# A delta-rule attention with an MLP behind it on one core: chunk 2's Gram matrix moves into its own activation buffer, chunk 0's masked products alternate row halves, and the first third of the instruction order is rearranged

## The chip, the cores and the metric

The kernel runs on one core of one Trainium2 chip. The metric is the device time in microseconds (us) of one launch. The kernel before was timed three times; the median is 257.81 us, and the runs lie between 257.49 and 259.07 us.

## What is computed

Four batches of eight heads hold sequences of 768 tokens with 48 features. Each head keeps a 48 x 48 state that every token reads and then corrects; the outputs of all heads go through a two-layer MLP (384 to 2048 to 384) with the tanh form of GELU.

```python
k_n = k / (np.linalg.norm(k, axis=-1, keepdims=True) + 1e-06)
for t in range(S):
    y[:, :, t] = q[:, :, t] @ state            # per batch and head
    v_old = state.T @ k_n[:, :, t]
    state = state + beta[t] * outer(k_n[:, :, t], v[:, :, t] - v_old)
x = y.transpose(0, 2, 1, 3).reshape(B * S, H * D)
out = gelu_tanh(x @ w_in) @ w_out
```

## The kernel before, in words

**Tiling.** The 768 tokens are cut into 12 chunks of 64. A chunk has two units (x = 0, 1), so there are 24 units; a unit holds 16 of the 32 batch-and-head pairs, eight of them over each half of the 128 partitions. Names in the text are operation.unit or operation.chunk: A4.0 is operation A4 of unit 0, V.0 is V of chunk 0.

**Stages of a chunk.** The recurrence inside a chunk becomes the inverse of a triangular 64 x 64 matrix per head.
- Loads (`load`, L473): four DMAs each of k, q and v. `norms` (L496 to L504): squares (sq), their sums (sum), root (pow), eps, reciprocal (inv).
- `prep`: normalised keys (kn or knc, L532 and L525) and queries (qb, qbc) as bf16, their transposes by TensorE (Tk, Tq, or T for both) and the copies out of PSUM (kTk, kTq, kT), the Gram matrix of the keys (GD or G, L565), its copy dn (L344), and the masked product of keys and queries (wq, or wqa with wqb).
- `leaf`: the 8 x 8 diagonal blocks are inverted by elementwise operations. F (L645) folds dn, lp and x0 start, L (L661) spreads, and then six pairs xm, xa (L667, L670) follow each other on DVE. xb multiplies the result with beta (bc, copied out by betaC).
- `scale`: xe or xec (L603, L600) spreads xb over a block-diagonal tile zt; GM makes the masked products, for chunk 0 directly from dn and zt (`direct`, L618 and L619), later from the keys by way of KZ and kz; lw (L635) selects from GM.
- `invert`: X10, X11 build the block-diagonal tile bd, and A4, rt4, B4, A5, rt5, B5 with copies into bd (bde40, bde41 or xi4 with bdc; be50, be51) raise it to the inverse of the whole chunk.
- `chain`: the one serial path from chunk to chunk, V, K, R, U, Un, S, Sn, and for the output Q, O, On; then the transpose of the output (X, xT, or a DMA, turnx).
- `mlp`: 16 products up (L837), four GELUs of four each (L841), 8 groups of four products down (L848), two copies Z and the stores.

**What sets the order.** A text table ORDER lists all operations in one sequence; `:p a d g s` names the engine (TensorE, ScalarE, VectorE, GpSimd, SyncE) and `@` the first PSUM bank. `Flow.order` deals the list out to the engines' queues, which run strictly in that order. `Flow.emit` gives each instruction waits on semaphores for those operations whose result it reads, whose buffer it overwrites, or whose PSUM bank it takes. GpSimd's operations on the upper and the lower half of the partitions also wait for one another. DMAs are issued by SP, ACT and GpSimd at their place in these queues. `fillN` is a 128 x 512 product of zeros whose result nobody reads; 37 of them stand in the table.

**Buffers.** dn, the bf16 copy of the Gram matrix, has two buffers that alternate by chunk (`dn[c % 2]`). gT, the activations of the MLP, has three (`gT[c % NG]`), each 16 x 256 elements per partition.

## Time and profile before

| What | Value |
|---|---|
| median of three runs | 257.81 us |
| the profiled execution, its own time | 256.19 us |
| its span from the first to the last instruction | 254.5 us |
| PE, DVE, ACT, POOL busy | 230.0, 186.5, 154.6, 136.6 us |
| first product up (up8.0) starts at | 48.86 us |

The profile lists engine time by line of the code. PE is TensorE's matmuls, PEld its weight loads, DVE VectorE, ACT ScalarE, POOL GpSimd, SP SyncE; a q behind a name is the queue that issues DMAs. A busy share is a mean over stages with different limits, so the stages are read one by one. DVE instructions that don't depend on each other overlap by up to 0.1 us in the records, so that the sum of their durations is a little more than the time that passes.

### The profile page before, as it was taken

What the parts mean: (1) busy time and instruction counts of PE and PEld (TensorE: products, weight loads), DVE (VectorE), ACT (ScalarE), POOL (GpSimd) and SP (SyncE); (2) the same over time, 40 slices, a digit from 0 to 9 for tenths busy, and PEclk for the clock granted to TensorE, in tenths of its full rate; (3) what the DMA queues carried; (4) which work ended last, traced back from release to release, by engine and by line L of the source; (5) the groups of instructions that cost most, each with busy time, mean ns of one, the idle gap of its engine ahead of it and who ended that gap; (6) DMA issues with size and microseconds to landing.
All of it is one profiled execution on the core that took longest, in us unless ns stands there. A gap on an engine that the chain in (4) does not pass through costs nothing.

```text
span 254.5 us, 12234 instructions
## 1 busy us (share of the span) xinstructions
PE 230.0 (90%) x5488; PEld 176.2 (69%) x5499; DVE 186.5 (73%) x448; ACT 154.6 (61%) x242; POOL 136.6 (54%) x160
## 2 busy tenths in 40 slices
PE   0286887799999999999999999999999999999994
PEld 0256656687776868777778787777786778678672
DVE  5896899998678989878888878898494765655100
ACT  0625757887577779768737687643958425436261
POOL 8646348977195397718257988463535526230000
PEclk9998999999999999999999999999999999999999
DMA  5999978989565679785777627687358220222042
GB/s 96 181 168 159 197 135 135 169 139 109 81 82 104 121 131 138 148 173 94 140 130 158 124 43 136 127 161 136 59 105 181 37 49 4 53 48 64 3 93 62
DMA packets 105332, 28.45 MB, mean 112 GB/s; under 512 B 99392, under 2 KB 104512, under 8 KB 105280
## 3 DMA queue, kind: packets, MB, share of 16 engines
q1 hardware_dynamic: 90288, 22.17, 50.8%
q0 software_dynamic: 2880, 3.15, 8.0%
q10 hardware_dynamic: 12112, 2.35, 6.2%
q8 instruction: 43, 0.70, 1.1%
q14 instruction: 9, 0.07, 0.1%
HBM read 20.64 MB, written 4.72 MB: 100 GB/s over the span
## 4 chain that ended last, share of the span: by engine, by line
PE 70%; DVE 13%; SPq 5%; POOL 3%; ACT 3%; DMA 2%; issue 2%; DVEq 0%
PE ps L848 24%; PE ps L837 22%; PE ps L705 5%; SPq L473 4%; PE ps L765 2%; DMA qraw<-in_q_dram 2%; PE ps L612 2%; PE ps L565 2%; PE ps L710 2%; ACT gT L841 2%; PE ps L772 2%; PE ps L645 2%; PE ps L786 2%; PE ps L628 1%; DVE lw L635 1%
## 5 line engine op out<-in xcount | busy, mean ns | idle before, releaser
L837 PE MATMUL ps<-xT,W 128*128 128x256 bf16 x576 | 75.2, 273 | 0.5 <-ACT gT L841 0.5
L848 PE MATMUL ps<-W,gT 128*128 128x384 bf16 x384 | 72.9, 326 | 0.0
L841 ACT ACTIVATE gT<-ps 128x1024 bf16<-128x1024 f32 x48 | 48.6, 1023 | 22.1 <-PE ps L837 21.7
L837 PEld LDWEIGHTS ps<-xT,W 128*128 128x128 bf16 x576 | 51.2, 97 | 8.7 <-ACT gT L841 0.6
L848 PEld LDWEIGHTS ps<-W,gT 128*128 128x128 bf16 x384 | 33.9, 97 | 18.2
L695 POOL TENSOR_SCALAR_AFFINE_SELECT bd<-lw 64x512 bf16<-64x512 bf16 x31 | 20.7, 672 | 27.6 <-DVE lw L635 23.3
L717 DVE TENSOR_TENSOR rl<-ps,two 128x384 bf16<-128x384 f32 (+1 forms) x48 | 22.8, 486 | 8.6 <-PE ps L705 8.2
L635 DVE CAST_PREDICATED lw<-mlw,ps 128x832 bf16<-128x832 uint16 x24 | 24.4, 1020 | 5.0 <-PE ps L612 4.8
L500 POOL TENSOR_TENSOR nrm<-nrm,half 128x16 f32<-128x16 f32 x9 | 26.7, 2969 | 1.6 <-DVE nrm L498 1.6
L344 ACT ACTIVATE bd<-ps 32x256 bf16<-32x256 f32 (+1 forms) x38 | 15.8, 424 | 8.9 <-PE ps L710 5.4
L705 PEld LDWEIGHTS ps<-lw,bd 128*128 128x128 bf16 x384 | 14.9, 96 | 5.4 <-DVE bd L697 1.0
L705 PE MATMUL ps<-lw,bd 128*128 128x48 bf16 (+1 forms) x384 | 16.8, 180 | 1.6 <-DVE bd L697 0.5
L735 POOL COPY bd<-xi 64x256 f32<-64x256 f32 x20 | 8.1, 403 | 16.3 <-ACT xi L344 8.4
L344 ACT ACTIVATE ob<-ps 128x384 f32<-128x384 f32 x17 | 8.3, 489 | 13.3 <-PE ps L848 13.2
L603 POOL TENSOR_TENSOR zt<-xb,blk 128x1024 bf16<-128x1024 bf16 x7 | 13.8, 1984 | 4.5 <-DVE xb L682 4.3
L670 DVE TENSOR_TENSOR xl<-ps,xl 128x96 bf16<-128x96 f32 (+3 forms) x66 | 14.7, 227 | 1.7
L667 DVE TENSOR_TENSOR ps<-ps,xl 128x96 f32<-128x96 f32 (+5 forms) x66 | 14.4, 221 | 2.1 <-PE ps L661 0.4
L350 ACT ACTIVATE kT<-ps 128x512 bf16<-128x512 f32 x16 | 9.3, 596 | 7.5 <-PE ps L628 7.5
L532 POOL TENSOR_TENSOR tok<-kraw,nrm 128x384 bf16<-128x384 f32 x7 | 7.2, 1032 | 11.4 <-DVE nrm L504 6.4
L600 POOL TENSOR_TENSOR zt<-xb,blk 128x2048 bf16<-128x2048 bf16 x3 | 10.9, 3641 | 4.1 <-DVE xb L682 3.9
L587 POOL TENSOR_TENSOR wq<-wq,muq 128x512 bf16<-128x512 bf16 x11 | 12.8, 1171 | 0.4
L344 DVE CAST bd<-ps 32x256 bf16<-32x256 f32 (+1 forms) x21 | 8.8, 422 | 5.3 <-ACT bd L344 3.1
(144 smaller groups left out, 441.2 us busy)
## 6 DMA issues: line engine op xcount, KB each, us to landing
out_dram<-ob SPq DMA_DIRECT2D x22, 192.0 KB, 3.1
vraw<-in_v_dram SPq DMA_DIRECT2D x43, 96.0 KB, 3.6
qraw<-in_q_dram SPq DMA_DIRECT2D x40, 96.0 KB, 3.6
kraw<-in_k_dram SPq DMA_DIRECT2D x38, 96.0 KB, 3.5
W<-in_moe_w_in_dram POOLq DMA_DIRECT2D x2, 768.0 KB, 8.6
W<-in_moe_w_out_dram POOLq DMA_DIRECT2D x2, 768.0 KB, 8.7
qraw<-in_q_dram ACTq DMA_DIRECT2D x8, 96.0 KB, 3.7
kraw<-in_k_dram ACTq DMA_DIRECT2D x6, 96.0 KB, 4.0
```

What stands on the lines that cost most here:

```text
L344: return e.activation(out, in_, ACT.Copy) if e is nc.scalar else e.tensor_copy(out, in_)
L500: if e is nc.scalar else e.tensor_tensor(nr[:, 1, hx], nr[:, 0, hx], half[:, hx], ALU.pow), reads=[nrn, "half"] + ["one"] * (c < ROOTS),
L603: A(("dve", "pool"), op("xe"), lambda e, P: e.tensor_tensor(zt[m][:, :, :].rearrange("p h (b j) -> p h b j", j=LB), xb[y][:, H * x:H * x + ...
L635: A(("dve",), op("lw"), lambda e, P: e.copy_predicated(lw[m][:, :, 0:LW - LB], mlw[:, :, :].rearrange("p w t -> p (w t)")[:, 16:16 + LW - ...
L667: A(("dve",), f"xm{m}.{c}", lambda e, P, m=m, w=w, part=part: e.tensor_tensor(part(P), P(f"L.{c}")[:, off[m]:off[m] + 2 * H * w].rearrange ...
L670: A(("dve",), f"xa{m}.{c}", lambda e, P, m=m, part=part: e.tensor_tensor(xl[y][:, :, m + 1:LB], part(P), xl[y][:, :, m + 1:LB], ALU.add), ...
L695: A(("pool", "dve"), op(f"X1{a}"), lambda e, P, src=lw[m][hf(a), :, LW - C:LW], dst=bd[b_][hf(a), :, hf(a)], a=a: e.affine_select(out=dst, ...
L705: ins = e.matmul(P(name)[:, C * h + c0:C * h + c1], bd[b_][:, h, :], rhs[:, h, :])
L717: A(("dve",), op(f"rt{i}"), lambda e, P, i=i, c0=c0, c1=c1, r_=r_: e.tensor_tensor(r_[:, 0:H, c0:c1], P(ps(f"A{i}")).rearrange("p (h t) -> ...
L837: ins = e.matmul(P(ph)[:, 256 * f:256 * f + 256].rearrange("p (x t) -> p x t", x=2), W1[:, j, 128 * (i + f):128 * (i + f) + 128], x_[:, :, ...
L841: A(("act",), f"gelu{i // 4}.{c}", lambda e, P, i=i, ph=ph: e.activation(g_[:, i:i + 4, :], P(ph).rearrange("p (f t) -> p f t", f=4), ACT. ...
L848: ins = e.matmul(P(po)[:, 0:DM], g_[:, f, 128 * b:128 * b + 128], W2[:, f, :], start=(f == 0), stop=(f == FC - 1))
```

## The change

The changed kernel computes the same. Four things differ in the code.

1. Chunk 2 writes its Gram matrix dn into the first quarter of gT[2], the buffer that later takes chunk 2's own activations, and not into dn[0], which chunk 0 has used. `dn` of units 4 and 5 then no longer waits for the readers of chunk 0's dn; the first GELU of chunk 2 gets a write dependence on it.
2. `direct`, the masked products of chunk 0, visits the two row halves (a) in turn instead of one half after the other.
3. bc of chunk 0 is copied without a change of sign, and xb.0 becomes the plain product that the other chunks use, so that GpSimd may take it.
4. ORDER differs. Up to the start of chunk 3 nearly every operation has another place, some another engine, form or bank; later the engines' queues differ in smaller steps and in the banks. 31 fills remain of 37.

```diff
 ORDER = """
-k1.00:a tmplz:g k0x1.11:s ident:g bdz1:d blk1:g blk2:g bdz3:d k0x1.01:a q0.00:s low1:d rowz:d ...
+v0.01:a k0x1.00:s pad1:g pad5:d pad0:g mmlw:d low1:d rpad0:g one:d tmplz:d half:d wz:g ...
...
-                    A(EV, f"betaC{i}", lambda e, P, i=i, d0=d0, d1=d1, w=w: neg(
+                    A(EV, f"betaC{i}", lambda e, P, i=i, d0=d0, d1=d1, w=w: (neg if i else copy)(
...
+        gram_of = [(dn[c % 2], c % 2) if c != 2 else (gT[2][:, 0:4, :].rearrange("p f (h t) -> p (f h) t", t=C), 2) for c in range(NC)]
...
-            d_, dnn = dn[c % 2][:, H * x:H * x + H, :], f"dn{c % 2}{x}"
+            d_, dnn = gram_of[c][0][:, H * x:H * x + H, :], f"dn{gram_of[c][1]}{x}"
...
             def direct(e, P):
                 for g in range(4):
-                    for p, a in quad:
+                    for p in range(2):
                         h, o_ = 4 * p + g, 512 * p + 2 * C * g
-                        e.matmul(P(ps("GM"))[hf(a), o_ + LW - C:o_ + LW - LB], zt[m][hf(a), h, hf(a)], d_[hf(a), h, 0:C - LB])
-                        ins = e.matmul(P(ps("GM"))[hf(a), o_:o_ + C - 16], d_[hf(a), h, :], zt[m][hf(a), h, C * a + 16:C * a + C])
+                        for a in range(2):
+                            e.matmul(P(ps("GM"))[hf(a), o_ + LW - C:o_ + LW - LB], zt[m][hf(a), h, hf(a)], d_[hf(a), h, 0:C - LB])
+                        for a in range(2):
+                            ins = e.matmul(P(ps("GM"))[hf(a), o_:o_ + C - 16], d_[hf(a), h, :], zt[m][hf(a), h, C * a + 16:C * a + C])
...
-            A(("dve",) if c == 0 else ("dve", "pool"), f"xb.{c}", lambda e, P: e.scalar_tensor_tensor(xb[y][:, :, :], xl[y][:, :, :], -1.0, bc[:, c, :, :], op0=ALU.mult, op1=ALU.mult) if c == 0 else
-              e.tensor_tensor(xb[y][:, :, :], xl[y][:, :, :], bc[:, c, :, :], ALU.mult),
+            A(("dve", "pool"), f"xb.{c}", lambda e, P: e.tensor_tensor(xb[y][:, :, :], xl[y][:, :, :], bc[:, c, :, :], ALU.mult),
...
-                  reads=["one"], frees=[ph], writes=[f"{gn}.{i // 4}"])
+                  reads=["one"], frees=[ph], writes=[f"{gn}.{i // 4}"] + ([f"dn2{x}" for x in range(2)] if c == 2 and not i else []))
```

`leaf` folds from `gram_of[c]` in the same way. How the instructions moved is shown at three places. Lines of the changed kernel are one to three higher than those of the kernel before.

**VectorE's queue at the very start.** bd are the block-diagonal tiles that have to be cleared once, kraw0 the raw keys of chunk 0, sq1 and nrm their squares and norms, tok0 the normalised keys (kraw1 those of chunk 1). Before:

```order
L422 MEMSET bd1 128x512
L422 MEMSET bd3 128x512
L397 MEMSET low0 128x1
L382 MEMSET rows0 128x512
L422 MEMSET bd0 128x512
L365 TENSOR_SCALAR identf0<-tmpl0 32x32
L422 MEMSET bd4 128x512
L344 COPY lw1<-tmpl0 128x896
L422 MEMSET bd5 128x512
L395 TENSOR_REDUCE unit0<-ident0 128x8
L497 TENSOR_TENSOR sq1<-kraw0 128x384
```

Now:

```order
L423 MEMSET bd0 128x512
L383 MEMSET rows0 128x512
L405 MEMSET tok0 128x16x8
L396 TENSOR_REDUCE unit0<-ident0 128x8
L366 TENSOR_SCALAR identf0<-tmpl0 32x32
L498 TENSOR_TENSOR sq1<-kraw0 128x384
L499 TENSOR_REDUCE nrm0<-sq1 128x8
L392 TENSOR_TENSOR own0<-blk0 128x64
L402 CAST xl0<-unit0 128x16
L405 MEMSET tok0 128x16x8
L393 TENSOR_TENSOR sel0<-ident0,own0 128x1024
```

Four of the five clears of bd have left the stretch ahead of the keys (bd1, bd3, bd4 and bd5 are GpSimd's now). The tile sel stands behind the first sum of squares and now behind own and blk, which GpSimd writes.

**VectorE's queue at the end of the first leaf.** xl0 and xl1 are the leaves of chunks 0 and 1, zt0 the spread tile, kT the copies of transposed queries, lw the selected products, bd0 and bd1 the tiles to invert. Before:

```order
L681 SCALAR_TENSOR_TENSOR xb0<-xl0,bc0 128x128
L603 TENSOR_TENSOR zt0<-xb0,blk0 128x1024
L344 COPY kT3<-ps 128x512
L667 TENSOR_TENSOR ps<-ps,xl1 128x16
L603 TENSOR_TENSOR zt0<-xb0,blk0 128x1024
L344 COPY kT2<-ps 128x512
L670 TENSOR_TENSOR xl1<-ps,xl1 128x16
L603 TENSOR_TENSOR zt0<-xb1,blk0 128x1024
L635 COPY_PREDICATED lw0<-mlw0,ps 128x8x104
```

Now:

```order
L673 TENSOR_TENSOR xl0<-ps,xl0 128x16
L351 TENSOR_SCALAR bc0<-ps 128x512
L601 TENSOR_TENSOR zt0<-xb0,blk0 128x2048
L684 TENSOR_TENSOR xb1<-xl1,bc0 128x128
L604 TENSOR_TENSOR zt0<-xb1,blk0 128x1024
L638 COPY_PREDICATED lw0<-mlw0,ps 128x8x104
L638 COPY_PREDICATED lw1<-mlw0,ps 128x8x104
L699 TENSOR_TENSOR bd0<-lw0,two0 64x8x64
L345 CAST gT2<-ps 128x512
L719 TENSOR_TENSOR rl0_0<-ps,two0 128x8x48
```

xb.0 has gone to GpSimd, both halves of its spread are one instruction, the copies kT have gone to ScalarE, betaC3 (bc0) and the Gram copy of unit 5 (gT2) have come from ScalarE, and unit 0 is inverted ahead of unit 1.

**ScalarE's queue from the chain of chunk 0 to the first GELU.** us0, st1 and xo0 are the results of U, S and O; L872 (L874 now) loads the table for the GELU. Before:

```order
L350 ACTIVATE rs0<-ps 128x768
L344 ACTIVATE bd1<-ps 32x8x32
L344 ACTIVATE bd0<-ps 32x8x32 x2
L344 ACTIVATE us0<-ps 128x768
L344 ACTIVATE bd3<-ps 64x8x64
L347 ACTIVATE bd3<-ps,low0 128x8x64
L344 ACTIVATE st1<-ps 128x768
L344 ACTIVATE xT0<-ps 128x768
L872 ACT_TABLE_LOAD
```

Now:

```order
L874 ACT_TABLE_LOAD
L874 ACTIVATE one0<-one0 128x1
L345 ACTIVATE bd1<-ps 64x8x64
L348 ACTIVATE bd1<-ps,low0 128x8x64
L351 ACTIVATE rs0<-ps 128x768
L345 ACTIVATE bd0<-ps 32x8x32 x2
L345 ACTIVATE bd1<-ps 32x8x32 x2
L345 ACTIVATE us0<-ps 128x768
L345 ACTIVATE xo0<-ps 128x2x8x48
L345 ACTIVATE st1<-ps 128x768
```

The table load stands ahead of the inversion of unit 1, On.0 (xo0) and the fourth copy of B5 (be51.1) have come from VectorE, and xT.0 has gone to VectorE.

## The prediction

> **What bounds the kernel now.** First I read the stretches of the span.

> ```profile
> core 0: us, PE busy (x) PEld busy (x) DVE busy (x) ACT busy (x) POOL busy (x), PEclk, DMA share, GB/s
> 0.00:20.00 20.00, 8.10 (x116) 5.20 (x117) 14.68 (x44) 6.59 (x13) 13.52 (x36) 1.00 1.14 149
> 20.00:48.90 28.90, 22.54 (x611) 17.14 (x620) 26.27 (x79) 19.45 (x38) 18.22 (x23) 0.94 0.98 156
> 48.90:60.00 11.10, 10.93 (x264) 8.96 (x264) 9.49 (x17) 8.44 (x12) 9.61 (x9) 1.00 1.00 139
> 60.00:100.00 40.00, 38.42 (x1093) 29.39 (x1090) 33.07 (x80) 30.81 (x52) 23.89 (x26) 1.00 0.67 110
> 100.00:240.00 140.00, 139.06 (x3338) 107.82 (x3338) 101.97 (x228) 84.46 (x126) 71.38 (x70) 1.00 0.54 100
> ```

> The columns are length, busy time of the five engines with their counts, granted clock and DMA. From 48.9 us on PE is idle for 0.17, 1.58 and 0.94 us in 191 us: that stage is a fixed sum of matmuls, and no other engine sets its end. Before it PE has gaps, some of its work is fills, and DVE is busy for 26.27 of 28.90 us. So the run ends a fixed time after the first product up, and what counts is when that starts. The chain of waits over this stretch says what leads there.

> ```profile
> 14.46 6.23 DMA qraw<-in_q_dram
> ...
> 20.71 0.36 DVE tok L344
> ...
> 34.33 0.94 DVE lw L635
> ...
> 46.35 0.82 DVE xo L344
> ...
> 48.93 1.09 PE ps L837 x9
> ```

> It comes out of the load of chunk 0's queries, which was issued at 14.46 and landed at 20.69, and then runs through DVE nearly without a break until the products up. DVE's other waits up to there:

> ```profile
> DVE tok L344 <- DMA qraw<-in_q_dram: 1.8, 1, 1.8
> ...
> DVE sq L497 <- DMA kraw<-in_k_dram: 0.9, 1, 0.9
> ```

> DVE is idle for 48.9 - 14.68 - 26.27 = 7.9 us before the first product up. The start of that product is therefore DVE's work ahead of it, plus these waits. Both sets of matmuls behind up8.0 are the same in the two orders but for A5.3 (it now stands behind) and three fills (two ahead of it now, one new one behind).

> **The change part by part.** *DVE's queue.* I compare what stands ahead of the products up, before with kz.4 as the next instruction, now with xT.0 included, since up8.0 now waits for it there. Prices are the means of groups up to 49 us:

> ```profile
> L603 DVE TENSOR_TENSOR zt<-xb,blk 128x1024 bf16<-128x1024 bf16 x4 | 2.8, 690 | 0.6 <-POOL xb L682 0.5
> L422 DVE MEMSET bd<- 128x512 f32 x5 | 2.4, 485 | 1.2 <-PEq L902 1.0
> ...
> L344 DVE COPY kT<-ps 128x512 bf16<-128x512 bf16 x5 | 2.1, 417 | 0.0
> ...
> L532 DVE TENSOR_TENSOR tok<-kraw,nrm 128x384 bf16<-128x384 f32 x3 | 1.6, 556 | 0.1
> L344 DVE CAST dn<-ps 128x512 bf16<-128x512 f32 x2 | 1.3, 680 | 0.0
> L697 DVE TENSOR_TENSOR bd<-lw,two 64x512 bf16<-64x512 bf16 x3 | 1.3, 419 | 0.1
> ...
> L344 DVE CAST xo<-ps 128x768 bf16<-128x768 f32 x1 | 1.0, 951 | 0.0
> ...
> L350 DVE TENSOR_SCALAR kT<-ps 128x512 bf16<-128x512 f32 x1 | 0.7, 692 | 0.1
> ...
> L344 DVE CAST bd<-ps 32x256 bf16<-32x256 f32 x1 | 0.4, 416 | 0.0
> ```

> and, for the two forms that come later in the run:

> ```profile
> L525 DVE TENSOR_TENSOR tok<-kraw,nrm 128x768 bf16<-128x768 f32 x2 | 1.9, 950 | 0.0
> L600 DVE TENSOR_TENSOR zt<-xb,blk 128x2048 bf16<-128x2048 bf16 x1 | 1.2, 1227 | 0.0
> ```

> Out: four clears of bd less one that comes ahead, 3 x 0.485 = 1.46; four copies kTq, 4 x 0.417 = 1.67; On.0 0.95; be51.1 0.42; three of X less two, 0.42; kn.2 and kn.3 as one knc.1, 2 x 0.556 - 0.950 = 0.16; xe.0 and xe.1 as one xec.0, 2 x 0.690 - 1.227 = 0.15; qb.1, bdc40.0 and rt5.3, together 1.15. Sum 6.38 us. In: dn.1 and dn.5, 2 x 0.680 = 1.36; betaC3, priced as the nearest copy of its size out of PSUM, 0.69; kn.0 0.56; xT.0, 768 elements of bf16, which is not in the rows of DVE and must cost more than the 0.417 of 512 elements and less than the 0.951 of 768 wider ones (I take 0.55, by the row of its type); small clears, templates and own, 0.9. Sum 4.06 us. DVE's work ahead of the first product falls by 2.3 us.

> *DVE's waits.* They do not stay as they are. The first keys come later: the last quarter of them is fifth in ACT's queue before, sixth in SP's now, at one issue per 0.68 us.

> ```profile
> 0.80 6.11 ACTq L473 DMA_DIRECT2D kraw<-in_k_dram  x9
> ...
> 6.60 0.99 DVE L497 TENSOR_TENSOR sq<-kraw 128x384 f32<-128x384 f32 x1 [0.93 <-DMA kraw<-in_k_dram]
> ```

> 0.79 + 5 x 0.68 = 4.2 against 0.80 + 4 x 0.68 = 3.5, so sq.0b starts at some 7.2 in place of 6.60, and the clears that filled the time ahead of it are gone. That puts about 2.6 us of idle time there (bounds 1.9, if the landing at 6.60 was not set by this quarter, and 3.0). Against that the wait of 1.8 for the queries goes: all four loads are issued by 11 us, three us earlier, and GpSimd converts them (bound: none of it goes, if the loads then land no earlier). The wait for xb.1 on GpSimd (0.5) goes as xb.1 comes to DVE; xb.0 on GpSimd is covered by betaC3's 0.69. A new one stands ahead of rt4.0: X10.0 waits on GpSimd behind xe.2 and a clear, and A4.0 behind it.

> ```profile
> 31.78 2.42 POOL L603 TENSOR_TENSOR zt<-xb,blk 128x1024 bf16<-128x1024 bf16 x1
> ```

> 2.42 + 0.5 + 0.7 = 3.6 us, and about 0.4 for A4.0 and the hand-offs, against 0.69 + 2 x 1.02 + 0.42 + 0.68 = 3.8 of DVE's own work with overlaps of 0.3: some 0.5 us is left (0 to 1.5). Waits in all: +2.6 - 1.8 - 0.5 + 0.5 = +0.8, rounded down to +0.7 for the smaller hand-offs that the merged spread saves. Net at the first product: -2.3 + 0.7 = -1.6 us, from 48.86 to 47.3.

> *Alternating row halves.* Two batches of `direct` and two of the later kind:

> ```profile
> L618 PE MATMUL ps<-dn,zt 64*64 64x56 bf16 x32 | 1.4, 192 | 0.2 <-ACT kT L344 0.2
> ...
> L612 PE MATMUL ps<-kT 48*64 48x56 bf16 x32 | 0.8, 194 | 0.4 <-ACT kT L350 0.4
> ```

> A batch takes 0.7 us now and could take 0.4, as the batch whose neighbours lie in different row halves does. I count nothing: DVE's xb.1 and xe.3 (1.0 us) cover GM.0, and lw.0 covers GM.1. Without that cover it saves 0.3 us once.

> *The room for chunk 2.* dn.5 started at 33.97 behind G.5, after the readers of chunk 0's buffer had ended at 32.3, and the order still has the GM of chunk 0 ahead of G.4: nothing, with nothing to cover.

> *ACT and PE.* ACT takes On.0 and the fourth copy of B5, and the table load leaves the path to the first GELU; it has 9.4 us free in the second stretch. A5.3 now costs 0.3 us behind up8.0, where PE is full, and the balance of fills gives back 0.2. Total: -1.6 + 0.1 = -1.5 us.

> *A rule against it.* The change has GpSimd and DVE work side by side more often. Two rows bear on that:

> ```profile
> 47.07 3.10 POOL L500 TENSOR_TENSOR nrm<-nrm,half 128x16 f32<-128x16 f32 x1
> ...
> 49.58 0.93 DVE L603 TENSOR_TENSOR zt<-xb,blk 128x1024 bf16<-128x1024 bf16 x1
> ```

> A DVE product of two tensors took 0.93 under a GpSimd one, 0.69 beside the start of xe.2. [...] Were that third added to knc.1, kn.1, kn.0 and xe.3, the gain would be 0.6 us instead of 1.5; xe.3 under xe.2 shows none of it, so the sum leaves it out.

> **The rivals.** *More is gained (about 3 us).* If the first keys are no later (idle 0.7 less), the wait ahead of rt4.0 is covered (0.5 less) and GM.0 shows its 0.3: -3.0, and the median is 254.8. For it: the keys share DMA engines that are busy anyway. Against it: the issue alone is 0.7 later.

> *The start eats it (no change, 257.8).* On PE Tq.1 stands ahead of Tk.0, GD.1, GD.0 and F.1, so that late queries now hold the Gram matrix too; and DVE has betaL1 and sum.2 ahead of the whole leaf, sum.2 needing keys of chunk 2 that ACT issues behind sq.0a. If either keeps 1.6 us of the old wait of 1.8, nothing is left. For it: the one load whose flight shows took 6.23 us. Against it: it was issued at 14.46, behind more traffic.

> *TensorE drops to half clock inside the inversions (slower, 259.4).* It has happened once here, between 20 and 30 us:

> ```profile
> 20.00:25.00 5.00, 3.27 (x68) 3.07 (x70) 3.86 (x14) 2.89 (x8) 3.55 (x8) 0.81 1.15 155
> 25.00:30.00 5.00, 4.50 (x65) 3.37 (x63) 4.72 (x25) 3.18 (x7) 1.47 (x1) 0.84 1.11 201
> ...
> 21.81 0.56 PE L457 MATMUL ps<-bhl,rows 128*128 128x48 bf16 x16
> ...
> 25.02 1.49 PE L457 MATMUL ps<-bhl,rows 128*128 128x16 bf16 x32
> ```

> 16 matmuls took 0.75 there against 0.56, for a shorter form: at least 0.2 per batch. Between A4.0 and X.0 some 15 batches stand in one line: 15 x 0.2 = 3.0, and -1.5 + 3.1 = +1.6. It ends slower than before once more than seven of them fall into it. There are six fills fewer; against it, PE is no emptier there than before, when the clock stayed at 1.00. [...]

> **How the numbers follow.** The profiled execution took 256.19 us, its span 254.5; the forecast for such an execution is 254.7, for the span 253.0. It lies 1.6 under the median, so the median goes from 257.81 to 256.3. Chances: forecast 0.50, more gained 0.20, start eats it 0.20, half clock 0.10. With all costs at their bad bounds (idle 0.4 more at the keys, the wait of 1.8 kept, 1.0 more at rt4.0, 0.4 on xT.0, against -1.5) the time is 259.9, with all at the good ones 254.6; I leave out the corners and give 254.2 to 259.2. A measurement of this kernel tells a change of about 1% (2.6 us) from none, that is 255.2 and 260.4. Most of the second case and the lower edge of the first lie below: faster 0.28. The worst of the half clock lies above: slower 0.08. Within 1%: 0.64.

> **What would show it.** Right: the first product up at 47.3 (46.5 to 48.1); DVE's wait for the queries gone and about 2.6 us of idle time ahead of sq.0b, near 7.2; DVE busy for some 39 us ahead of that product; PE idle for under 3 us between it and the last 15 us. Wrong: an xm1.1 later than 23.5, a granted clock under 1 after 30 us, or a PE that waits for ACT between 47 and 60 us.

## The result, and the profile after

The changed kernel is slower by about 1%: 260.6 us median of 15 runs (258.64 to 261.95) against 258.05 us for the kernel before on the same chips (255.56 to 259.11); ratio 1.0106, 95% interval 1.0071 to 1.014. I had forecast 256.3, with a range up to 259.2. The profiled execution took 260.2 us, its span 258.5 (before 256.19 and 254.5). Ratios here and below are taken over the fast runs alone, those within 1.5% of the kernel's fastest, so that they can differ a little from the quotient of the medians.

The stretches of the span of the changed kernel, as before them in the prediction:

```profile
core 0: us, PE busy (x) PEld busy (x) DVE busy (x) ACT busy (x) POOL busy (x), PEclk, DMA share, GB/s
0.00:20.00 20.00, 7.93 (x68) 4.26 (x69) 12.61 (x39) 5.50 (x11) 13.82 (x37) 1.00 1.09 150
20.00:48.90 28.90, 20.24 (x524) 15.92 (x530) 23.50 (x71) 17.73 (x34) 16.51 (x21) 0.82 0.77 125
48.90:60.00 11.10, 9.40 (x227) 7.32 (x230) 9.28 (x21) 7.19 (x11) 7.77 (x9) 1.00 0.92 141
60.00:100.00 40.00, 38.83 (x1097) 30.43 (x1096) 32.67 (x80) 29.61 (x47) 25.45 (x27) 1.00 0.74 119
100.00:240.00 140.00, 139.22 (x3458) 108.96 (x3460) 105.78 (x236) 86.66 (x129) 74.43 (x74) 1.00 0.58 104
```

From 60 us on nothing has changed: TensorE (PE) is idle for 1.17 and 0.78 us. The loss lies ahead of it. Between 20 and 48.9 us VectorE (DVE) is busy 2.8 us less than before, and the clock is 0.82 and not 0.94. The chain of waits names the place:

```profile
34.67 0.42 PE ps L566 x16
35.19 1.95 issue
37.14 0.32 PE ps L631 x13
37.49 0.60 ACT kT L351
...
43.48 0.56 DVE rl L719
...
52.42 0.57 DVE xT L345
53.03 0.83 PE ps L839 x6
```

The first product up starts at 53.03; it was at 48.86 before, and I had forecast 47.3. From there to the end of the span 205.5 us pass, before 205.6: the whole loss of 4.2 us is made by 53 us. That is the difference of two single executions; the medians differ by 2.6 us, and the profiled execution of the kernel before lies 1.9 us under its median. So the figures below say where the time of these executions went, and the ratios say what an edit is worth. In the chain stands a piece of 1.95 us called issue, in which TensorE waited for nothing that the profile shows. Its own timeline there:

```profile
34.67 0.42 PE L566 MATMUL ps<-kT 48*64 48x128 bf16 x16 [0.25 <-issue]
34.97 0.22 PE L631 MATMUL ps<-zt,tok 64*64 64x64 bf16 x3
37.14 0.29 PE L631 MATMUL ps<-zt,tok 64*64 64x64 bf16 x13 [1.95 <-issue]
38.14 0.61 PE L428 MATMUL ps<-wz 128*128 128x512 bf16 x2 [0.71 <-ACT kT L351]
```

L631 is KZ.3, sixteen small products without a semaphore between them. TensorE stops after the third. A wait on another engine cannot stand there; what is left is that the next instruction was not there. Two more such gaps follow, inside GM.4 (1.02 us, until 55.02) and inside S.1 (0.78 us, until 70.04). The kernel before has no such gap of over half a microsecond inside an operation. The profile's list of DMA queues and two windows of the DMA view show the supply; the columns are packets, megabytes and share of the 16 engines. First the whole execution, then 30.7 to 34.7 us, then 34.7 to 35.0 us:

```profile
q8 instruction: 43, 0.70, 1.1%
```

```profile
q0 software_dynamic: 312, 0.64, 92.8%
q1 hardware_dynamic: 333, 0.06, 9.7%
```

```profile
q0 software_dynamic: 26, 0.05, 93.2%
q8 instruction: 1, 0.02, 19.2%
q1 hardware_dynamic: 27, 0.01, 15.8%
```

43 fetches bring 0.70 MB, 16 KB each, and TensorE has 10,976 loads and products, 255 to a fetch: I take these for its instructions, fetched in blocks. The gaps fit that: from the end of the first to the end of the second TensorE makes 758 loads and products, from there to the end of the third 762, and three fetches start in each of these stretches. With TensorE's semaphore instructions, of which the trace has 80, it is 764 and 768, and by this I estimate a block at 256 instructions. From 30.7 to 34.7 us, while q0, the weight load w1.1, holds 93% of the DMA engines, no fetch moves. One starts at 34.73, 0.46 us before TensorE stands still, and 2.4 us after its start TensorE goes on.

Behind the gap the clock falls:

```profile
35.00:40.00 5.00, 2.04 (x66) 1.41 (x62) 2.02 (x5) 3.05 (x6) 2.67 (x5) 0.93 0.64 115
40.00:45.00 5.00, 4.65 (x148) 3.72 (x137) 4.14 (x10) 3.56 (x7) 2.26 (x3) 0.50 0.85 151
45.00:50.00 5.00, 3.72 (x84) 2.70 (x87) 4.51 (x16) 3.62 (x8) 4.02 (x5) 0.88 0.65 89
```

TensorE is busy for 2.04 of the 5 us around the gap, and then runs at half clock from 39.3 to 46.2, through both inversions. The trace's record of the clock runs in steps of 3.41 us. In the step that ends where the half clock begins (35.93 to 39.34) TensorE is busy for 1.49 us. VectorE's waits show the rest:

```profile
DVE sq L498 <- DMA kraw<-in_k_dram: 5.0, 1, 5.0
DVE rl L719 <- PE ps L707: 3.8, 3, 2.9
```

The first keys cost 5.0 us of waiting (0.9 before, 2.6 forecast), and the wait ahead of rt4.0, which I had put at 0.5 us, is 2.9. The wait for the queries (1.8 before) is gone, as forecast.

### The profile page after: what moved, and what is told of

Read it like the earlier page. It is cut to its first block, busy times and chain, and to the rows that moved or that the text cites. A ratio compares the mean times of both kernels' runs of the same rounds, so it can differ in the third digit from the quotient of the medians.

```text
span 258.5 us, 12219 instructions
## 1 busy us (share of the span) xinstructions
PE 230.6 (89%) x5483; PEld 177.3 (69%) x5493; DVE 184.9 (72%) x444; ACT 153.1 (59%) x238; POOL 138.0 (53%) x165
## 3 DMA queue, kind: packets, MB, share of 16 engines
HBM read 20.64 MB, written 4.72 MB: 98 GB/s over the span
## 4 chain that ended last, share of the span: by engine, by line
PE 79%; DVE 11%; issue 3%; ACT 2%; DMA 2%; SPq 1%; POOL 0%; ACTq 0%
PE ps L839 25%; PE ps L850 24%; PE ps L707 5%; PE ps L613 3%; PE ps L767 3%; PE ps L566 3%; PE ps L788 2%; PE ps L712 2%; PE ps L631 2%; PE ps L648 2%; PE ps L774 2%; PE ps L810 2%; DMA kraw<-in_k_dram 2%; PE ps L797 1%; DVE rl L719 1%
## 5 line engine op out<-in xcount | busy, mean ns | idle before, releaser
L843 ACT ACTIVATE gT<-ps 128x1024 bf16<-128x1024 f32 x48 | 48.5, 1022 | 22.5 <-PE ps L839 22.3
L697 POOL TENSOR_SCALAR_AFFINE_SELECT bd<-lw 64x512 bf16<-64x512 bf16 x34 | 22.9, 678 | 33.3 <-DVE lw L638 27.0
L345 ACT ACTIVATE bd<-ps 32x256 bf16<-32x256 f32 (+1 forms) x35 | 14.6, 423 | 7.0 <-PE ps L707 3.5
L670 DVE TENSOR_TENSOR ps<-ps,xl 128x96 f32<-128x96 f32 (+4 forms) x66 | 14.4, 221 | 2.3 <-PE ps L664 1.0
L588 POOL TENSOR_TENSOR wq<-wq,muq 128x512 bf16<-128x512 bf16 x13 | 15.8, 1218 | 0.6
L673 DVE TENSOR_TENSOR xl<-ps,xl 128x96 bf16<-128x96 f32 (+5 forms) x66 | 14.7, 228 | 1.8
L604 POOL TENSOR_TENSOR zt<-xb,blk 128x1024 bf16<-128x1024 bf16 x6 | 11.9, 1994 | 5.4 <-DVE xb L684 5.3
L345 DVE CAST bd<-ps 32x256 bf16<-32x256 f32 (+1 forms) x23 | 9.5, 421 | 5.3 <-ACT bd L345 3.3
L428 PE MATMUL ps<-wz 128*128 128x512 bf16 x21 | 9.1, 487 | 4.2 <-POOL wz L357 1.5
```

Of the source, the lines that this page charges most:

```text
L345: return e.activation(out, in_, ACT.Copy) if e is nc.scalar else e.tensor_copy(out, in_)
L588: A(("pool",), op("wqb"), lambda e, P: e.tensor_tensor(wq[s][:, :, :], wq[s][:, :, :], muq[:, :].unsqueeze(1).to_broadcast([128, H, C]), A ...
L670: A(("dve",), f"xm{m}.{c}", lambda e, P, m=m, w=w, part=part: e.tensor_tensor(part(P), P(f"L.{c}")[:, off[m]:off[m] + 2 * H * w].rearrange ...
L673: A(("dve",), f"xa{m}.{c}", lambda e, P, m=m, part=part: e.tensor_tensor(xl[y][:, :, m + 1:LB], part(P), xl[y][:, :, m + 1:LB], ALU.add), ...
L697: A(("pool", "dve"), op(f"X1{a}"), lambda e, P, src=lw[m][hf(a), :, LW - C:LW], dst=bd[b_][hf(a), :, hf(a)], a=a: e.affine_select(out=dst, ...
L843: A(("act",), f"gelu{i // 4}.{c}", lambda e, P, i=i, ph=ph: e.activation(g_[:, i:i + 4, :], P(ph).rearrange("p (f t) -> p f t", f=4), ACT. ...
```

## The experiments

My theory after this: TensorE starved for instructions inside KZ.3, because w1.1, which the new order issues at 28.8 us and not at 24.0, lay in the way of the fetch; the half clock followed from the gap; and the late first keys are a second, separate loss. The rivals: too little work on TensorE halves the clock whatever the gap, or the late keys are the whole loss. Ratios are to the kernel before, run on the same chip.

**w1_early.** The load moved back:

```diff
-  sq.2:g ... w1.0:g ... eps.2:g ... qbc.2:g ... w1.1:g first1:g
+  sq.2:g ... w1.0:g w1.1:g ... eps.2:g ... qbc.2:g ... first1:g
```

> The changed kernel, with one load moved: the second half of the up weights (w1.1) stands directly behind the first half (w1.0) in GpSimd's queue, ahead of eps.2, so that its bytes have passed by some 30 us. Theory (TensorE starves for instructions): the fetch of the next block of instructions no longer waits behind this load, the gap of 2.0 us inside KZ.3 is gone, A4.0 starts at about 36.3 and not 38.4, the clock stays at 1.00 from 30 us on because the gap is what halved it, and the first product up starts at 48.4 (47.5 to 49.3) and not 53.0; the time falls by 4 to 5 us, to 0.99 to 1.00 of the kernel before. Rival 1 (too little work on TensorE around the first inversion halves the clock, whatever the gap): the gap goes, the half clock stays, first product at 51, time 2 us less, about 1.002. Rival 2 (the late start of the first keys is the loss): first product above 52, time within 0.7 of the changed kernel, about 1.01.

Measured: 256.3 us (255.26 to 258.8), ratio 0.9975 (0.9942 to 1.0007). Its timeline at the same place, its window from 40 to 45 us, and VectorE's wait ahead of rt4.0:

```profile
35.21 0.32 PE L631 MATMUL ps<-zt,tok 64*64 64x64 bf16 x16
36.52 0.61 PE L428 MATMUL ps<-wz 128*128 128x512 bf16 x2 [0.99 <-ACT kT L351]
36.97 0.36 PE L707 MATMUL ps<-lw,bd 128*128 128x48 bf16 x8
```

```profile
40.00:45.00 5.00, 4.11 (x139) 3.01 (x136) 4.93 (x15) 4.27 (x8) 4.21 (x5) 1.00 0.32 54
```

```profile
DVE rl L719 <- PE ps L707: 1.0, 1, 1.0
```

All sixteen products run through: the fetch for the block that begins among them starts at 31.75, 0.7 us after TensorE enters the block before it. The clock stays at 1.00, and the first product up starts at 49.89, 3.1 us earlier. That is less than expected (48.4, at the latest 49.3), and so is the gain, some 3.4 us by the ratios and not 4 to 5. The step of the clock's record around the gap's old place (34.70 to 38.11) has 2.07 us of busy TensorE. The order of TensorE's work is the same, so the half clock does not come from it: the first rival falls. The first keys are as late as before (8.58), so the second falls as the whole cause.

**pad_blocks.** No load moves; only the ends of the blocks do:

```diff
-fill96@0 ...
+fill96@0 pat0@0 pat1@0 pat2@0 pat3@0 ...     # 8 products of zeros each, 64x64 by 64
```

> The changed kernel, with 32 small products of zeros (64x64 by 64) added at 2 us, where TensorE is idle; no load and no other engine is touched. They move the ends of the blocks of 256 instructions 64 instructions up the program. Theory (starvation): the block that was asked for at 30.8 is now asked for at about 26.5, between the two weight loads, and is there in time; no gap inside KZ.3, clock 1.00 from 30 us on, first product up at 48.4 (47.5 to 49.8, the later if a smaller gap of up to 1 us comes near 39), time 3.5 to 5 us less than the changed kernel, about 0.99 to 1.00 of the kernel before. Rivals 1 and 2: nothing that they name has changed; time within 0.5 us of the changed kernel, about 1.01.

Measured: 257.39 us, ratio 0.9993 (0.9965 to 1.0021). Adding 32 useless products makes the changed kernel 1.1% faster, some 2.9 us, where 3.5 to 5 were expected. KZ.3 runs through, and the smaller gap that was allowed for near 39 us is there, inside GM.3:

```profile
38.87 0.40 PE L622 MATMUL ps<-kT 48*64 48x56 bf16 x25
40.21 0.24 PE L622 MATMUL ps<-kT 48*64 48x56 bf16 x7 [0.94 <-issue]
```

```profile
40.00:45.00 5.00, 3.81 (x126) 2.88 (x129) 4.38 (x11) 3.81 (x6) 3.24 (x4) 1.00 0.80 141
```

The first product starts at 51.10, later than expected. Here a gap of 0.94 us left the clock alone; the step of the clock's record around it (37.14 to 40.55) has 2.25 us of busy TensorE.

**keys_first.** The second loss by itself:

```diff
-v0.01:a k0x1.00:s ... beta01:s ... k0x1.10:s ... k1.01:s ... k0x1.01:s ... k0x1.11:s
+v0.01:a k0x1.00:s k0x1.10:s k0x1.01:s k0x1.11:s ... beta01:s ... k1.01:s
```

> The changed kernel, with the four loads of the keys that sq.0b reads (k0x1) first in SP's queue, as DMA 1 to 4 and not 1, 3, 5 and 6. Theory (starvation): sq.0b starts at 6.9 to 7.2 and not 8.55, the leaf comes 0.7 earlier because sum.1 then waits for its own squares and not for the tile sel; the weight load and the block of instructions move along, so the gap inside KZ.3 stays at about 2 us and the half clock behind it too; time 0.7 less, 1.007 of the kernel before. Rival 2 (the late keys are the loss): first product up 2 us earlier or more, time 2 us less or more, 1.003 or under.

Measured: 257.59 us, ratio 0.9989 (0.9953 to 1.0025). This is what the second rival had forecast (1.003 or under), and the first product up starts at 50.52, 2.5 us earlier, which is its forecast too. The gap inside KZ.3 is still there, as the theory said, but the gain is 3 us and not 0.7:

```profile
32.80 0.22 PE L631 MATMUL ps<-zt,tok 64*64 64x64 bf16 x3
35.33 0.29 PE L631 MATMUL ps<-zt,tok 64*64 64x64 bf16 x13 [2.31 <-issue]
```

sq.0b starts at 6.51, inv.1 1.0 us earlier, but xm1.1 2.1 us earlier (23.24 for 25.39). The difference lies in two VectorE instructions. In the changed kernel, VectorE and GpSimd (POOL) side by side, and then the same VectorE instruction with keys first:

```profile
18.25 1.46 DVE L420 TENSOR_SCALAR rl<-tmpl 128x128 bf16<-128x128 bf16 x1
```

```profile
18.18 1.48 POOL L498 TENSOR_TENSOR sq<-kraw 128x768 f32<-128x768 f32 x1 [0.93 <-DVE bsb L351]
```

```profile
16.89 0.19 DVE L420 TENSOR_SCALAR rl<-tmpl 128x128 bf16<-128x128 bf16 x1
```

An instruction of 0.19 us took 1.46 where it met sq.2 on GpSimd. kn.1 takes 1.05 beside the conversion qbc.0 and 0.55 without it. Together that is 1.77 us, which vanished here by timing alone. The half clock was shorter as well, 3.4 us (36.2 to 39.6) and not 6.8. So the late keys cost time of their own, and they are not the whole cause: w1_early and pad_blocks gain as much with the keys as late as before. How the 3 us divide between the keys, the collisions and the shorter half clock is not shown.

**keys_and_w1** is both moves together.

> The changed kernel with both earlier moves together: the four loads of k0x1 first in SP's queue, and w1.1 directly behind w1.0. Theory (two separate losses: late first keys with what they collide with, 2 to 2.6 us, and the starved TensorE with the half clock behind it, 3 to 4.5 us): the two gains add up but for a rest; the first product up starts at 47.6 (47.2 to 48.3; the later end if the block asked for near 28.7 still comes behind the weights, whose bytes pass until 30.8), time 2.3 us less than with w1.1 alone, 0.989 of the kernel before (0.986 to 0.992). Rival (both moves took away the same loss, and the first inversion is then held by GpSimd or VectorE): first product at 49.5 or later, 0.996 to 1.000.

Measured: 256.63 us, ratio 0.9995 (0.9967 to 1.0023). The gains did not add: the time, and a first product up at 49.54 where 47.6 was expected, are those of the rival. Its mechanism, a first inversion held by GpSimd or VectorE, did not show: the leaf ends early, and the first weight load of A4.0 starts at 34.95, 1.8 us before w1_early. Instead the starving moved on, to GM.2, and to GM.4 (0.88 us), with a half clock behind the first:

```profile
38.48 0.25 PE L613 MATMUL ps<-kT 48*64 48x56 bf16 x8
39.86 0.38 PE L613 MATMUL ps<-kT 48*64 48x56 bf16 x24 [1.13 <-issue]
```

```profile
40.00:45.00 5.00, 4.39 (x122) 3.27 (x116) 3.88 (x11) 3.00 (x6) 4.94 (x6) 0.69 0.46 62
```

The fetch for that block started at 37.11, 3.4 us after TensorE had entered the block before it, and no weight load was on its way then. So this fetch was as late without one; what held it is not shown.

**keys_w1_pad** adds the 32 products of pad_blocks to that.

> The same, with the 32 small products of zeros at 2 us, so that the ends of the blocks move 64 instructions up. Theory: should the kernel without them still have a gap inside KZ.3, it is gone here, the block being asked for at about 24.5 and needed at about 32; first product up at 47.3 (46.9 to 48.0), time equal to that kernel's or up to 1 us less, 0.987 of the kernel before (0.984 to 0.991). Rival: as for the kernel without them, equal within 0.3 us in any case.

Measured: 254.96 us (253.19 to 258.19), ratio 0.9906 (0.9865 to 0.9947). This version beats both kernels. There is no gap inside an operation of the first inversions but one of 0.40 us in A5.1 (42.39, its fetch started at 39.59), and the first product up starts at 48.52, 0.5 us later than the bound I had given. The 32 products are worth some 2.3 us here, more than the 1 us that was allowed for them:

```profile
20.00:48.90 28.90, 20.93 (x606) 16.24 (x613) 24.94 (x75) 19.61 (x38) 19.11 (x22) 0.94 0.93 149
48.90:60.00 11.10, 11.08 (x287) 9.16 (x284) 10.08 (x21) 8.76 (x11) 9.70 (x11) 1.00 0.84 140
```

**old_order** is the code of the changed kernel with the ORDER text of the kernel before.

> The code of the changed kernel (chunk 2's Gram matrix in the activations, alternating row halves, the sign of bc) with the order of the kernel before. All theories: these three edits are worth nothing here; GM.0 and GM.1 take 0.58 to 0.60 us each as before, first product up at 48.9 (48.6 to 49.1), time within 0.3 us of the kernel before, 0.999 to 1.001. Were the alternation worth what I allowed for it, GM.0 and GM.1 would take 0.3 to 0.4 each.

Measured: 256.56 us, ratio 0.9986 (0.9957 to 1.0016). The three edits of the code are worth nothing that can be measured; the whole difference is in the order. Its profiled execution took 260.17 us, far above this median, and shows that the order of the kernel before can starve as well. The fetch starts at 48.60, behind the load of down weights; TensorE stops inside KZ.4, and the first product up, expected at 48.9, starts at 51.16:

```profile
47.98 0.28 PE L631 MATMUL ps<-zt,tok 64*64 64x64 bf16 x11 [0.30 <-DVE zt L604]
50.91 0.31 PE L631 MATMUL ps<-zt,tok 64*64 64x64 bf16 x5 [2.65 <-issue]
```

How often that happens in either kernel was not counted.

**before_w1_late, before_pad72, w1_late_k3_first and before_pad** try to make the kernel before starve. The first has w1.1 behind knc.2 and 72 small products behind betaT0:

```diff
-betaT0@0 ... w1.1:g ... knc.2:g
+betaT0@0 pat0@2 ... pat8@2 ... knc.2:g w1.1:g
```

> The kernel before, with w1.1 behind knc.2 in GpSimd's queue (issued at about 28.5, where the changed kernel has it) and 72 small products of zeros (64x64 by 64) behind betaT0 on TensorE, which only move the places where one block of 256 instructions ends. Theory (starvation): the block that ends near 36 us is asked for at about 31, waits for the weight load and comes at about 37, so that TensorE stands still for 0.5 to 2 us between 35 and 38 in the middle of an operation; the time rises by 0.5 to 2 us, and by up to 4 if the clock halves behind it. Rival (the weights are not needed before 48 us and the products lie in idle time): no gap inside an operation, time within 0.5 us of the kernel before.

Measured: 263.99 us, ratio 1.0245 (1.0199 to 1.0291): slower by more than the theory's upper end, and not in the way it said. There is no gap inside an operation between 35 and 38 us. The fetch of the block that ends there did start 3.5 us after TensorE entered the block before, where it was 0.2 us without the late load, but TensorE was slow enough to need it only 2.7 us later. The clock is half from 48.5 to 55.3 here too, with no such gap ahead of it: in the step before, TensorE was busy for 1.81 of 3.41 us. What the queue view shows is SP:

```profile
SPq L483 <- DMA W<-in_moe_w_in_dram: 10.0, 1, 10.0
```

SP held k4.00 until w1.1 had landed (w1 is declared a reader of that buffer), and chunk 3's keys stood behind it. I took that for the cause and tested it by moving two of these loads ahead, and tested the products alone.

```diff
-k4.00:s ... q3.10:s ... k3.11:s ... k4.10:s ... k3.10:s
+k3.10:s k3.11:s k4.00:s ... q3.10:s ... k4.10:s
```

> The kernel before with w1.1 late and the 72 small products, as in before_w1_late, and two loads of chunk 3's keys (k3.10, k3.11) ahead of k4.00 in SP's queue. Theory now (no starved TensorE there: the loss was SP, which waited 10.0 us at k4.00 for the weight load, since that load is declared a reader of the buffer that k4 overwrites; chunk 3's keys stood behind it, and behind them sq.3, sum.3 and On.0): sq.3 starts at 43 or earlier and not 45.6, first product up at 49.9 (49.4 to 50.4) and not 51.6, no half clock behind it, time 1.003 to 1.006 of the kernel before. Rival (the late weight load costs by itself, by bandwidth or by a late block of instructions): first product still at 51 or later, 1.015 or more.

> The kernel before with the 72 small products behind betaT0 and nothing else. Theory: they hold betaT1 and with it VectorE by some tenths and shift the ends of the blocks; first product up 0.3 to 1.0 us late (49.2 to 49.9), no gap inside an operation ahead of it, time 1.001 to 1.005 of the kernel before. Rival (the small products, not the late load, made before_w1_late slow): 1.015 or more.

Measured: w1_late_k3_first 264.42 us, ratio 1.0258 (1.0193 to 1.0324); before_pad72 261.87 us, ratio 1.0186 (1.0117 to 1.0255). Both expectations of the theory fail. sq.3 no longer waits for its keys, yet it starts at 44.55 and not by 43 (in before_pad72, where no load is late, at 45.05), and the first product up starts at 51.36. And the 72 products alone, which run from 9.5 to 11.6 us where TensorE had waited until 11.2, make the kernel 1.9% slower; what the late load adds lies within the intervals. The trace of before_pad72 shows two places. ScalarE starts the copies of transposed keys at 20.32 and not 18.43, behind a DMA issue of 3.36 us (1.41 before):

```profile
16.91 3.36 ACTq L482 DMA_DIRECT2D vraw<-in_v_dram  x1
20.32 1.09 ACT L344 ACTIVATE kT<-ps 128x512 bf16<-128x512 bf16 x2 [5.79 <-issue]
```

Chunk 0's queries land 2.5 us later too, and the first product up starts 3.0 us late. Then, where TensorE was idle for 0.94 us of 140 before, it is idle for 3.4, with gaps of 0.3 to 0.6 us inside GM.10, K.7 and O.9 as a part of it:

```profile
100.00:240.00 140.00, 136.56 (x3405) 106.53 (x3391) 104.41 (x231) 84.88 (x127) 72.80 (x72) 1.00 0.59 104
```

I take the gaps of the second for ends of blocks in other places; no fetch is shown for them. For the first, the fetch that used to start at 21.7 now starts at 16.1, among the first loads; that this is what holds them is argued, not shown. The two other kernels with these products have the fetch as early (15.7 and 16.1), and the copies start at 18.93 and 19.45 there, the queries land 1.0 and 1.1 us late: the size changes from one execution to the next.

The last one puts 112 small products ahead of betaT0:

```diff
-bdz1:d ... wz:g ... betaT0@0
+wz:d bdz1:d ... pat0@2 ... pat13@2 betaT0@0
```

> The kernel before, with 112 small products of zeros (64x64 by 64) ahead of betaT0 on TensorE, where it is idle (the tile of zeros is cleared first on VectorE for it, in place of GpSimd). No load is moved. Theory (starvation): the blocks of 256 instructions now end 224 instructions earlier in the program, one of them among the operations at 34 us; it is asked for at about 29, waits for the weight load whose bytes pass until 32.8, starts at 31 to 33 and is there 2.4 us later, so that TensorE stands still for 0.4 to 1.6 us in the middle of an operation near 34; the first product up 0.5 to 1.5 later than 48.86, more if the clock halves; time 1.002 to 1.012 of the kernel before. Rival (the gap in the changed kernel has another cause): no gap, time within 0.3 us of the kernel before.

Measured: 258.74 us, ratio 1.0055 (1.0024 to 1.0086), inside the expected range, first product at 49.84. The gap came at the place foretold, with 0.31 us smaller than foretold:

```profile
33.87 0.64 PE L575 MATMUL ps<-kT 48*64 48x64 bf16 x30
34.82 0.24 PE L575 MATMUL ps<-kT 48*64 48x128 bf16 x2 [0.31 <-issue]
```

It was not what made this kernel late: xm1.1 was 0.7 us late already, and A4.1 0.6. So the place of the gap bears the theory out, while the time lies in the range in good part by luck.

**All gaps together.** For the gaps above, the time from the start of the block's fetch (queue q8) to TensorE's next instruction:

| Kernel, operation | gap, us | fetch starts | TensorE goes on | between |
|---|---|---|---|---|
| changed, KZ.3 | 1.95 | 34.73 | 37.14 | 2.4 |
| changed, GM.4 | 1.02 | 52.65 | 55.02 | 2.4 |
| changed, S.1 | 0.78 | 67.72 | 70.04 | 2.3 |
| keys_first, KZ.3 | 2.31 | 32.86 | 35.33 | 2.5 |
| pad_blocks, GM.3 | 0.94 | 37.45 | 40.21 | 2.8 |
| keys_and_w1, GM.2 | 1.13 | 37.11 | 39.86 | 2.8 |
| keys_and_w1, GM.4 | 0.88 | 49.06 | 51.38 | 2.3 |
| keys_w1_pad, A5.1 | 0.40 | 39.59 | 42.39 | 2.8 |
| old_order, KZ.4 | 2.65 | 48.60 | 50.91 | 2.3 |
| before_pad, G.5 | 0.31 | 32.28 | 34.82 | 2.5 |

A block is there 2.3 to 2.8 us after its fetch starts, and every one of these gaps ends then. Counted over nine traces (all but old_order, before_pad72 and w1_late_k3_first), a fetch starts, in the median, 1.2 us after TensorE enters the block before (315 fetches after 60 us), 1.6 us in the busy first 60 us (38 fetches), and 3.2 us while a weight load fills the DMA engines (22 fetches). By these medians and the 2.4 us of the table I estimate that a block of TensorE has to last some 4 us, or 5.6 beside a weight load, if the next one is to be there in time. In the changed kernel the block that ends in KZ.3 had been entered at 30.8 and was used up at 35.0, in 4.2 us; the blocks around this place lasted 7.0 and 5.6 us in the kernel before.

## Why the prediction was wrong

The sign was wrong. By its own steps:

- *"That stage is a fixed sum of matmuls", the run ends a fixed time after the first product up.* Right for these two: 205.5 us against 205.6. In the other traces it is 203.9 (w1_early) to 210.6 us (w1_late_k3_first); gaps (0.3 to 0.6 us inside GM.10, K.7 and O.9 of before_pad72) and half clock (48.5 to 55.3 in before_w1_late) fall into that stretch as well.
- *DVE's work ahead of that product falls by 2.3 us, to some 39.* About right. It was busy for 39.8 us up to 53.03, against 40.9 up to 48.86; of that the collisions with GpSimd are 1.77, in the kernel before 0.63 (betaL1 took 0.96 in place of 0.33). Without them it falls by 1.1 + 1.1 = 2.2 us, where 2.3 were forecast.
- *The first keys: sq.0b at 7.2, 2.6 us of idle time, at most 3.0.* The term was mis-sized, and the bound with it: 8.55 and 5.0 us. The last quarter was issued at 4.56 and not 4.2, and took 4.0 us to land and not 3.0. keys_first gets 3.0 us back, the collisions and one window of half clock included.
- *Some 0.5 us left ahead of rt4.0 (0 to 1.5).* This is the step that failed. It was worked out from GpSimd's queue and took it that TensorE issues A4.0 when its inputs are there. It was 2.9 us, since TensorE had no instructions: every wait of the sum was the wait for a result, and TensorE's own supply was put at nothing without a reason. In w1_early, where the gap is gone, the wait is 1.0, inside the range. The half clock behind the gap is the second price of the same step.
- *A rule against it: a DVE product took a third longer under a GpSimd one (0.93 for 0.69).* I priced it at 0.9 us and left it out, because xe.3 under xe.2 showed nothing. It came to 1.14 us net, at ladj4.1 (1.46 for 0.19), which I had not looked at, and at kn.1 (1.05 for 0.55). kn.1 reads two inputs and ladj4.1 one; what makes an instruction slow beside GpSimd no run here shows.
- *The rival of the half clock, chance 0.10, 259.4 us.* Its time came nearest to the 260.6 us, but by luck: the measured loss also holds the gap, the late keys and the collisions, and no run separates what the half clock alone cost. I argued that PE is no emptier than before; it was emptied by the gap, and w1_early, with the same work in the same order on TensorE, keeps the clock at 1.00.
- *The start eats it.* In part right, but not by the queries or by sum.2: the new order lost 2.2 us at xm1.1 (25.39 for 23.23, later than the 23.5 that I had named as the sign of being wrong), by the keys and the collisions.
- *Alternation and chunk 2's room: nothing.* Right: old_order 0.9986; the form with 56 columns takes 1.3 us for its 32 products, 1.4 before.

The balance at the first product up: 47.3 forecast, 53.03 measured, 5.7 us too late. Of that 3.1 go when TensorE no longer starves (w1_early, 49.89), and 1.4 more when the keys come first and the blocks end well (keys_w1_pad, 48.52). 1.2 us remain that my sum promised and no version delivered. In keys_w1_pad the first weight load of A4.0 starts at 34.92, 1.3 us before the first A4 of the kernel before (36.22), but the second A4 follows 2.9 us later and not 1.9, and the last B5 ends at 43.55 against 43.27: the lead is lost between the two inversions. Which of the operations that now stand between them on TensorE costs it was not tried.

## What to carry to other kernels

## What was not expected of the hardware

- The order of the work alone does not set the time: 32 idle products gave 1.1% back to the changed kernel (1.0106 to 0.9993), 72 cost the kernel before 1.9%.
- A weight load on the software queue held 93% of the DMA engines from 30.7 to 34.7 us, and the 16 KB fetch at 34.73 started 3.95 us after TensorE had entered the block before it.
- One gap of 1.95 us, with 0.71 behind it, was followed by 6.8 us of half clock, one of 1.13 by 3.4 us; gaps of 0.94 and 1.02 us were followed by none. The steps of 3.41 us ahead of four half clocks had 0.54 (keys_first), 1.49 (changed), 1.80 (keys_and_w1) and 1.81 us (before_w1_late) of busy TensorE, those of w1_early and pad_blocks around the same work 2.07 and 2.25; what decides between them these traces do not settle.
- A VectorE instruction of 0.19 us took 1.46 beside a GpSimd product of 1.48.
